# A delta-rule attention and a two-layer MoE in one kernel: the second layer with still tokens and moving weights, and a new order of norms, inversion and start

## The chip, the cores and the metric

The kernel runs on one core of one Trainium2 chip. The metric is the time of one execution on the device in microseconds (us). TensorE is called PE, VectorE DVE, ScalarE ACT, GpSimd POOL; SP is the engine that issues the DMAs here.

## The reference, cut to what matters

```python
# q, k, v: (4, 8, 768, 48); beta: (4, 8, 768); w_in: (384, 2048); w_out: (2048, 384)
k_n = k / (norm(k) + 1e-6)
for t in range(768):
    y[:, :, t] = q[:, :, t] @ state
    v_old = state.T @ k_n[t]
    state = state + beta[t] * outer(k_n[t], v[t] - v_old)
x = y.transpose(0, 2, 1, 3).reshape(3072, 384)
h = x @ w_in
g = maximum(h, 0) + log1p(exp(-abs(h)))
out = g @ w_out
```

## The kernel before, in words

**Attention.** The 768 tokens are cut into 12 chunks `s` of 64, two chunks make a pair `u`. All 32 heads of a chunk are worked on together, two heads side by side on the 128 partitions. For each pair the norms of k are taken (`norms`, L143: square on ACT, row sum on DVE L154, logarithm and exponential on ACT, then a chain of small DVE steps that ends with `cT`, `ncT`), the products k·k of each chunk (`gram`, L112), and the inverse of a unit lower triangular 32x32 matrix per head (`invert`, L180). The inversion is DVE work: one transposition (L193), two multiplications (L197, L199), then a step per column, each a multiplication into a scratch tile (L216) and an addition (L222). `finish` (L225) transposes the result twice (L228, L229). Pairs 0 and 1 invert 16x16 blocks and put them together on PE (`join`, L232). Then per chunk: `cross_a`, `cross_b`, `k_state`, `p_half` with `mask_p` (DVE L301), `u_all`, `y_all` (PE L333, then the split of y into two fp32r halves by ACT L337 and DVE L339, L341, then six small DMAs x<-x), and `state`.

**MoE.** Each chunk's 256 tokens go through both layers. The hidden 2048 features are 16 blocks `f`, taken two at a time, which is called a group here: eight groups per chunk. Numbers are kept as a sum of two fp32r parts, so each product is three matmuls. The first layer has w_in as the still operand and 256 token columns as the moving one, 18 matmuls per group (L428). ACT does three passes (L432 to L434), DVE three (L435, and the split into `gh` and `gl` by L438 and L439). The second layer (`outp`, L410) has 128 columns of w_out as the still operand and 256 token columns of `gh` or `gl` as the moving one, again 18 matmuls per group, into `po`, which holds the whole chunk in three banks. ACT copies `po` out and SP stores it. The first layer's PSUM tile `ph` has two buffers: a group's matmuls must wait until L435 of the group two before it is done.

**Weights.** They come as 64-bit floats. Each of the 16 blocks is converted by six DVE and ACT steps (`weights`, L354: ACT L366, DVE L372, L375, L378, L381, ACT L384, DVE L368, for the last block L386).

**Order.** Up to the end of the block at L508 the engines other than SP run in the order of the code. After it a planner writes the order: `attention` is a generator whose steps are let through by `attend` as the MoE goes on (`target`, with RATE, LEAD, FIRST), and a scheduler orders each engine's instructions from that. On each engine the instructions then run in that fixed order, SP's DMAs too. `prepare` (L464) did norms, gram and the whole inversion of the next pair in one go, after the even chunk. The tile `nv` (two buffers) holds v and, for the norms, k.

Of the kernel before, what the change touches and what calls it, by code (L numbers as in the profile page):

```python
# [34 lines left out]
def deltanet_moe(ctx, tc, kT, qT, kN, kI, vN, beta, wts, out):  # L35
# [7 lines left out]
    ps_a = E(tc.tile_pool(name="ps_a", bufs=3, space=PSUM))  # L43
# [68 lines left out]
    def gram(s):  # L112
        if s not in OFF:
            OFF[s] = two.tile([P, NP, HB], F32, name="off")
# [20 lines left out]
    def gram_below(s):  # L135
        OFF[s] = two.tile([P, NP, HB], F32, name="off")
# [6 lines left out]
    def norms(u, kas=None):  # L143

        ss = one.tile([P, 2 * NP], F32, name="ss")
        for j in range(2):
            if kas is None:
                ka = two.tile([P, NP, D], F32, name="nv")
                nc.sync.dma_start(ka, kN[2 * u + j])
            else:  # L150
                ka = kas[:, j]
            nc.scalar.activation(ka, ka, AF.Square)
            yield
            nc.vector.tensor_reduce(ss[:, j * NP:(j + 1) * NP], ka, op=ALU.add, axis=AX.X)  # L154
            yield
# [24 lines left out]
    def invert(u, cT, ncT):  # L180
# [22 lines left out]
        if u < N16:  # L203
# [5 lines left out]
            tmp = one.tile([P, HB, HB], F32, name="x0" if u == 0 else "x3")  # L209
        else:  # L210
            tmp = one.tile([P, HB, HB], F32, name="work")
# [113 lines left out]
    def y_all(s):  # L325
        x = X[s] = one.tile([P, 2, NK, B, C], F32R, name=f"x{s % 4}")
# [27 lines left out]
    def weights():  # L354
# [4 lines left out]
        ex = None  # L359
        for f in range(NF + 1):  # L360
            last, lastex = f - 1, ex
            if f < NF:
                w = ST[f].rearrange("p (n w) -> p n w", w=2)
                hw, lw = w[:, :, 1], w[:, :, 0]
                ex = two.tile([P, 2 * DM], I32, name="ex", bufs=3)
                nc.scalar.activation(ex.bitcast(F32), hw.bitcast(F32), AF.Abs)  # L366
                if f > 0:
                    nc.vector.tensor_tensor(W[last][:, 1], lastex.bitcast(F32), W[last][:, 0],  # L368
                                            op=ALU.subtract)
                    done[0] = f  # L370
                    yield
                nc.vector.tensor_scalar(ex.bitcast(F32), ex.bitcast(F32), 2.0 ** -15, 122880.0,  # L372
                                        op0=ALU.max, op1=ALU.min)
                yield
                nc.vector.tensor_scalar(ex, ex, 3, 0x3FFFFFF8, op0=ALU.logical_shift_left,  # L375
                                        op1=ALU.bitwise_and)
                yield
                nc.vector.scalar_tensor_tensor(ex, hw, -2 ** 30, ex, op0=ALU.bitwise_and,  # L378
                                               op1=ALU.bitwise_or)
                yield  # L380
                nc.vector.scalar_tensor_tensor(ex, lw, 29, ex, op0=ALU.logical_shift_right,  # L381
                                               op1=ALU.bitwise_or)
                W[f] = one.tile([P, 2, 2 * DM], F32R, name=f"w{f}")
                nc.scalar.copy(W[f][:, 0], ex.bitcast(F32))  # L384
            else:
                nc.vector.tensor_tensor(W[last][:, 1], lastex.bitcast(F32), W[last][:, 0],  # L386
                                        op=ALU.subtract)
                done[0] = f
            yield


    def moe():
# [115 lines left out]
    with tc.manual_schedule(engines={ET.PE, ET.DVE, ET.Activation, ET.Pool}):  # L508
# [6 lines left out]
        for f in range(2):  # L515
            load_weights(f)
# [174 lines left out]
```

## Time and profile before

| | us |
|---|---|
| median of 3 runs | 715.94 (714.91 to 717.95) |
| the profiled execution, its own time | 715.12 |
| its span in the profile | 713.4 |
| PE busy, matmuls | 621.8 |
| DVE busy | 452.6 |
| ACT busy | 351.7 |
| DVE busy, of the first 160 us | 120.0 |
| PE idle, of the first 80 us | 47.5 |

The span is what the profile covers of one execution; 1.7 us of the execution's own time lie outside it. Busy times of PE are modelled, since matmuls are pipelined, so its idle time is the better guide. A window row reads: from and to in us, its length, then for PE, PEld (the load of still operands), DVE, ACT and POOL the busy us and the number of instructions, the TensorE clock that was granted (1.00 is full), the DMA share and GB/s. A waits row reads: engine, line and tile that waited, on whom, us in total, how often, the longest.

### The profile page before, as it was taken

To read this page: it belongs to the slowest core of one execution; us is meant where nothing else is said; L and a number is where in the kernel's file an instruction comes from. 1 tells how busy PE (TensorE), PEld (TensorE's weight loads), DVE (VectorE), ACT (ScalarE), POOL (GpSimd) and SP (SyncE) were. 2 spreads that over 40 slices of the span, in tenths; PEclk is the share of its full clock that TensorE was granted. 3 is DMA by queue.
4 is the path that set the end of the run, shared out by engine and by line. 5 is a ranking of instruction groups with operands and counts; after the bars stand their busy time and mean duration, and the time that the engine had idled before them with its cause. 6 is when DMAs were issued, how large, how long until landed. Compare 5 with 4: busy or idle time off the path is not lost.

```text
span 713.4 us, 25301 instructions
## 1 busy us (share of the span) xinstructions
PE 621.8 (87%) x11392; PEld 594.9 (83%) x11392; DVE 452.6 (63%) x972; ACT 351.7 (49%) x651; POOL 28.5 (4%) x56
## 2 busy tenths in 40 slices
PE   3226879879998699999899999999798999999997
PEld 2226779778988698999799998899798989999996
DVE  1683799994454994465995449973679853534443
ACT  3304758634565246465346664463545555444443
POOL 4000000000000000000001000010000100000000
PEclk9999779899999899999999999999899999999999
DMA  9991212000042013041120312202302103000000
GB/s 245 374 374 35 58 45 59 1 1 27 3 112 59 1 46 79 2 119 53 46 57 26 106 44 69 57 2 91 79 3 48 55 3 80 2 12 23 2 23 22
DMA packets 36699, 45.36 MB, mean 64 GB/s; under 512 B 21648, under 2 KB 28688, under 8 KB 36592
## 3 DMA queue, kind: packets, MB, share of 16 engines
q1 hardware_dynamic: 36592, 43.76, 21.1%
q8 instruction: 89, 1.46, 0.9%
q14 instruction: 18, 0.15, 0.1%
HBM read 36.67 MB, written 4.72 MB: 58 GB/s over the span
## 4 chain that ended last, share of the span: by engine, by line
PE 57%; DVE 21%; ACT 9%; issue 7%; DMA 5%; SPq 1%; ACTq 0%; DVEq 0%
PE ph L428 21%; PE po L410 21%; PE pa L333 3%; DVE Z L222 3%; DVE work L216 2%; DMA nv<-kN 2%; PE pa L294 2%; DVE a L435 2%; PE pa L308 2%; ACT tt L265 1%; PE pa L320 1%; ACT a L432 1%; ACT a L433 1%; DVE gl L439 1%; PE pa L123 1%
## 5 line engine op out<-in xcount | busy, mean ns | idle before, releaser
L428 PE MATMUL ph<-x,w 128*128 128x256 f32 x1728 | 243.7, 293 | 20.1 <-DVE a L435 13.0
L428 PEld LDWEIGHTS ph<-x,w 128*128 128x128 f32 x1728 | 224.9, 197 | 24.3 <-DVE a L435 13.6
L410 PE MATMUL po<-gh,w 128*128 128x256 f32 x1152 | 179.1, 291 | 12.2 <-DVE gh L438 10.8
L410 PEld LDWEIGHTS po<-gh,w 128*128 128x128 f32 x1152 | 154.5, 193 | 16.0 <-DVE gh L438 9.6
L435 DVE SCALAR_TENSOR_TENSOR a<-ph,a 128x512 f32<-128x512 f32 x96 | 66.1, 689 | 158.0 <-ACT a L434 157.6
L432 ACT ACTIVATE a<-ph 128x512 f32<-128x512 f32 x96 | 57.2, 597 | 192.6 <-PE ph L428 185.9
L410 PE MATMUL po<-gl,w 128*128 128x256 f32 x576 | 103.1, 288 | 1.1 <-ACT ex L414 0.9
L410 PEld LDWEIGHTS po<-gl,w 128*128 128x128 f32 x576 | 84.0, 193 | 2.1 <-ACT ex L414 1.3
L439 DVE TENSOR_TENSOR gl<-a,gh 128x512 fp32r<-128x512 f32 x96 | 66.3, 690 | 4.2 <-PE po L410 1.8
L433 ACT ACTIVATE a<-a 128x512 f32<-128x512 f32 x96 | 60.5, 632 | 2.9
L434 ACT ACTIVATE a<-a 128x512 f32<-128x512 f32 x96 | 60.6, 632 | 2.7
L438 DVE CAST gh<-a 128x512 fp32r<-128x512 f32 x96 | 42.3, 441 | 7.4 <-PE po L410 4.0
L222 DVE TENSOR_TENSOR Z<-Z,work 128x30 f32<-128x30 f32 (+14 forms) x120 | 39.6, 330 | 2.9
L216 DVE TENSOR_TENSOR work<-Z,ltq 128x30 f32<-128x30 f32 (+14 forms) x120 | 39.5, 329 | 2.7
L333 PE MATMUL pa<-big 128*64 128x64 f32 x768 | 29.1, 235 | 4.3 <-DVE big L301 4.1
L333 PEld LDWEIGHTS pa<-big 128*64 128x64 f32 x768 | 26.5, 148 | 6.7 <-DVE big L301 4.6
L301 DVE TENSOR_TENSOR big<-pa,maskP 64x512 f32<-64x512 f32 x44 | 30.1, 685 | 0.8 <-PE pa L294 0.3
L323 ACT COPY big<-pa 48x384 f32<-48x384 f32 x44 | 20.8, 473 | 18.1 <-PE pa L320 17.4
L294 PE MATMUL pa<-big,kt 48*64 48x64 f32 x704 | 25.7, 224 | 3.1 <-ACT tt L277 2.3
L294 PEld LDWEIGHTS pa<-big,kt 48*64 48x64 f32 x704 | 23.2, 139 | 4.4 <-ACT tt L277 3.3
L267 POOL MEMSET tt<- 32x512 f32 x24 | 12.6, 524 | 311.2 <-ACT tt L265 201.3
L312 ACT COPY big<-pa 64x384 f32<-64x384 f32 x48 | 22.6, 470 | 3.2 <-PE pa L308 2.5
(96 smaller groups left out, 611.9 us busy)
## 6 DMA issues: line engine op xcount, KB each, us to landing
w<-wts SPq DMA_DIRECT2D x16, 768.0 KB, 13.2
kt<-kT SPq DMA_DIRECT2D x26, 192.0 KB, 4.4
big<-qT SPq DMA_DIRECT2D x24, 192.0 KB, 4.4
ki<-kI SPq DMA_DIRECT2D x24, 192.0 KB, 3.3
nv<-vN SPq DMA_DIRECT2D x12, 384.0 KB, 3.6
out<-ex SPq DMA_DIRECT2D x11, 384.0 KB, 2.6
nv<-kN SPq DMA_DIRECT2D x8, 384.0 KB, 3.5
x<-x SPq DMA_DIRECT2D x72, 32.0 KB, 2.0
```

The source lines that it names most:

```text
L216: nc.vector.tensor_tensor(tmp[:, a:a + r, 0:j], Z[:, a + j + 1:a + n, a + j:a + j + 1].to_broadcast([P, r, j]), lq[:, a + j:a + j + 1, a:a ...
L222: nc.vector.tensor_tensor(z, z, tmp[:, a:a + r, 0:j], op=ALU.add)
L294: nc.tensor.matmul(pt[tk[ab], i, :], kts[s % 3][dr[ab], 8 * g + i, :], bv[dr[ab], ab, 8 * g + i, 0:C], start=True, stop=True)
L333: nc.tensor.matmul(py[tk[ab], i, :], big[:, at + C:at + 2 * C], big[:, at:at + C], start=True, stop=True)
L410: nc.tensor.matmul(po[:, e, 0:n], W[f][:, a, DM + e * P:DM + (e + 1) * P], (gh, gl)[b][:, f - f0], start=(f == 0 and i == 0), stop=(f == N ...
L428: nc.tensor.matmul(ph[:, f - f0], W[f][:, a, k * P:(k + 1) * P], xr[b][k], start=(c == 0), stop=(c == 3 * NK - 1))
L432: nc.scalar.activation(a, ph, AF.Abs)
L433: nc.scalar.activation(a, a, AF.Exp, scale=-1.0)
L434: nc.scalar.activation(a, a, AF.Ln, bias=1.0)
L435: nc.vector.scalar_tensor_tensor(a, ph, 0.0, a, op0=ALU.max, op1=ALU.add)
L438: nc.vector.tensor_copy(gh, a)
L439: nc.vector.tensor_tensor(gl, a, gh, op=ALU.subtract)
```

## The change

Second layer: the still operand is now 128 of the chunk's tokens out of `gh` or `gl`, the moving one 384 columns of w_out. A block `f` takes 6 matmuls of 384 columns instead of 9 of 256. `po` needs two banks, the free one goes to the attention's pool `ps_a` (3 to 4 buffers). The last group of each chunk does one half of the tokens first, copies it out (128x384) and stores it, then the other.

Norms: the tile `nv` has three buffers. `chunk(s)` for even `s` from 2 on loads k and begins the norms of the next pair before its own work, ends them after the first `p_half`, and does the two grams of the next pair at its end. `load_v` is called a chunk earlier.

Inversion: it is handed to a list, `background`, from which the planner takes two pieces after each step of the MoE; what is left is taken when `finish` needs it. X has three buffers instead of four.

Start: the first inversion's norms, inversion and `finish` come without weight conversions between them; weight blocks 2 to 15 are loaded behind a small POOL memset of each (so after POOL's earlier work), pair 1's gram and norms are done in the start. The conversion steps are emitted in another order (the absolute value of the next block between two steps of this one, the subtraction of the last one after the second step).

```diff
-    ps_a = E(tc.tile_pool(name="ps_a", bufs=3, space=PSUM))
+    ps_a = E(tc.tile_pool(name="ps_a", bufs=4, space=PSUM))
...
-        NV[s] = two.tile([P, NP, D], F32, name="nv")
+        NV[s] = two.tile([P, NP, D], F32, name="nv", bufs=3)
...
+    def load_ka(s):
+        ka = two.tile([P, NP, D], F32, name="nv", bufs=3)
+        nc.sync.dma_start(ka, kN[s])
+        return ka
...
-        x = X[s] = one.tile([P, 2, NK, B, C], F32R, name=f"x{s % 4}")
+        x = X[s] = one.tile([P, 2, NK, B, C], F32R, name=f"x{s % 3}")
...
-            po = ps_o.tile([P, NK, 512], F32, name="po")
+            po = ps_o.tile([P, 2, 512], F32, name="po")
...
-                terms = [(f, i, e) for f in range(f0, f0 + 2) for i in range(3) for e in range(NK)]
-                last = f0 + 2 == NF and s == NS - 1
-                if last:
-                    terms.sort(key=lambda t: (t[1] == 2, t[2]))
+                terms = [(f, h, i) for f in range(f0, f0 + 2) for h in range(2) for i in range(3)]
                 if f0 + 2 == NF:
-                    ot = two.tile([P, NK, n], F32, name="ex", bufs=3)
+                    terms.sort(key=lambda t: t[1])
+                    ot = two.tile([P, 2, DM], F32, name="ex", bufs=3)
...
-                    nc.tensor.matmul(po[:, e, 0:n], W[f][:, a, DM + e * P:DM + (e + 1) * P],
-                                     (gh, gl)[b][:, f - f0], start=(f == 0 and i == 0),
+                    nc.tensor.matmul(po[:, h, 0:DM], (gh, gl)[b][:, f - f0, h * P:(h + 1) * P],
+                                     W[f][:, a, DM:], start=(f == 0 and i == 0),
...
+                    if f == NF - 1 and i == 2:
+                        nc.scalar.copy(ot[:, h], po[:, h, 0:DM])
+                        nc.sync.dma_start(out[s, h], ot[:, h])
...
     def chunk(s):
+        more = s % 2 == 0 and s + 2 < NS
         if s % 2 == 0:
             scale_v(s)
+            if more and s >= 2:
+                load_k(s + 2)
+                nm = norms(s // 2 + 1)
+                next(nm)
+            yield from begin(s)
         k_state(s)
         mask_p(0, p_half(s, 0))
         yield
+        if more and s >= 2:
+            cols[s // 2 + 1] = run(nm)
         u_all(s)
         mask_p(1, p_half(s, 1))
...
+        if more and s >= 2:
+            u = s // 2 + 1
+            systems(u)
+            load_k(s + 3)
+            gram(s + 2)
+            yield
+            gram(s + 3)
+            yield
+            background.append(invert(u, *cols[u]))
...
-        fill(2)
-        next(nm)
-        fill(2)
-        cols[0] = run(nm)
-        pts = [p_half(0, g, ps_h, "ph") for g in range(2)]
-        run(invert(0, *cols[0]))
+        pts = [p_half(0, g, ps_h, "ph") for g in range(2)]
         gram_below(1)
+        for f in range(2, NF):
+            ST[f] = one.tile([P, 4 * DM], I32, name=f"w{f}")
+            nc.gpsimd.memset(ST[f][:, 0:1], 0)
+            nc.sync.dma_start(ST[f], wts[f])
+            if f == 5:
+                load_k(3)
+        run(iv)
+        systems(1)
+        gram(2)
         finish(0)
...
+            if s % 2 == 0:
+                while background:
+                    yield "invert"
+                finish(s // 2)
+                yield
...
         while next(mg) != "chunk":
             groups += 1
+            invert_some(2)
             attend(0, target())
```

How the change moves DVE's instructions is shown at three places. In the rows a name is written ahead of `<-` and the names read behind it; numbers behind a name count tiles.

**DVE right after the first chunk's y.** Before, behind the last subtraction L341 of chunk 0 (`ex` and `w` are the conversion, `nv` is v, `a` the MoE):

```order
L91 TENSOR_TENSOR nv<-nv,nn 128x768
L378 SCALAR_TENSOR_TENSOR ex<-w_108,ex 128x768
L381 SCALAR_TENSOR_TENSOR ex<-w_108,ex 128x768
L368 TENSOR_TENSOR w_1047<-ex,w_1047 128x768
L372 TENSOR_SCALAR ex<-ex 128x768 x2
L375 TENSOR_SCALAR ex<-ex 128x768 x2
L372 TENSOR_SCALAR ex<-ex 128x768
L378 SCALAR_TENSOR_TENSOR ex<-w_110,ex 128x768
L378 SCALAR_TENSOR_TENSOR ex<-w_114,ex 128x768
L375 TENSOR_SCALAR ex<-ex 128x768
L381 SCALAR_TENSOR_TENSOR ex<-w_110,ex 128x768
L435 SCALAR_TENSOR_TENSOR a<-ph,a 128x512
```

In the change, six instructions behind the same subtraction (now L340), with the norms of pair 1 (`r_1125`) and, in L155, of pair 2:

```order
L383 SCALAR_TENSOR_TENSOR ex<-w_104,ex 128x768
L96 TENSOR_TENSOR nv<-nv,nn 128x768
L164 RECIPROCAL r_1125<-rt 128x32
L194 STREAM_TRANSPOSE ltq<-work 128x32x32
L165 TENSOR_TENSOR r_1125<-r_1125,ss 128x32
L166 TENSOR_TENSOR r_1125<-r_1125,rt 128x32
L155 TENSOR_REDUCE ss<-nv 128x16
L167 TENSOR_SCALAR nn<-r_1125 128x32
L171 TENSOR_TENSOR r_1125<-nn 128x32
L96 TENSOR_TENSOR nv<-nv,nn 128x768
L172 RECIPROCAL r_1125<-r_1125 128x32
L173 TENSOR_TENSOR r_1125<-r_1125,bet 128x32
```

The conversion of the third block stood here before; now the second block's stands among the norms of two pairs and the scaling of v, and the first L437 (L435 before) comes later in the list.

**DVE at the inversion of pair 2.** Before, from the L435 that precedes it:

```order
L435 SCALAR_TENSOR_TENSOR a<-ph,a 128x512
L193 STREAM_TRANSPOSE ltq<-work 128x32x32
L438 CAST gh<-a 128x512
L197 TENSOR_TENSOR ltq<-ltq,Z 128x1024
L439 TENSOR_TENSOR gl<-a,gh 128x512
L199 TENSOR_TENSOR Z<-ltq,cT 128x1024
L288 TENSOR_TENSOR nv<-nv,pa 128x8x48
L212 COPY Z<-cT 128x32
L216 TENSOR_TENSOR work<-Z,ltq 128x30
L288 TENSOR_TENSOR nv<-nv,pa 128x8x48
L222 TENSOR_TENSOR Z<-Z,work 128x30
```

In the change:

```order
L437 SCALAR_TENSOR_TENSOR a<-ph,a 128x512
L440 CAST gh<-a 128x512
L441 TENSOR_TENSOR gl<-a,gh 128x512
L194 STREAM_TRANSPOSE ltq<-work 128x32x32
L198 TENSOR_TENSOR ltq<-ltq,Z 128x1024
L200 TENSOR_TENSOR Z<-ltq,cT 128x1024
L211 COPY Z<-cT 128x32
L215 TENSOR_TENSOR work<-Z,ltq 128x30
L287 TENSOR_TENSOR nv<-nv,pa 128x8x48
L177 STREAM_TRANSPOSE cT<-r_4042 128x32
L221 TENSOR_TENSOR Z<-Z,work 128x30
```

The group's own casts moved ahead of the transposition; the inversion's first ten columns still follow in one stretch, with no MoE step among them.

**DVE at the norms of pair 3.** Before, from the second mask of the even chunk:

```order
L301 TENSOR_TENSOR big<-pa,maskP 64x8x64 x2
L154 TENSOR_REDUCE ss<-nv 128x16 x2
L159 TENSOR_SCALAR rt<-ss 128x32
L435 SCALAR_TENSOR_TENSOR a<-ph,a 128x512
L163 RECIPROCAL r_4569<-rt 128x32
L438 CAST gh<-a 128x512
L164 TENSOR_TENSOR r_4569<-r_4569,ss 128x32
L439 TENSOR_TENSOR gl<-a,gh 128x512
L165 TENSOR_TENSOR r_4569<-r_4569,rt 128x32
L339 TENSOR_TENSOR x_4373<-pa,x_4373 128x3x128
L341 TENSOR_TENSOR x_4374<-pa,x_4374 128x128
```

In the change, at the second mask of chunk 2:

```order
L300 TENSOR_TENSOR big<-pa,maskP 64x8x64 x2
L155 TENSOR_REDUCE ss<-nv 128x16 x2
L160 TENSOR_SCALAR rt<-ss 128x32
L164 RECIPROCAL r_4042<-rt 128x32
L165 TENSOR_TENSOR r_4042<-r_4042,ss 128x32
L338 TENSOR_TENSOR x_2769<-pa,x_2769 128x3x128
L340 TENSOR_TENSOR x_2770<-pa,x_2770 128x128
L166 TENSOR_TENSOR r_4042<-r_4042,rt 128x32
L96 TENSOR_TENSOR nv<-nv,nn 128x768
L437 SCALAR_TENSOR_TENSOR a<-ph,a 128x512
```

The same norms now stand one pair earlier, the two row sums still directly behind one another, and the next MoE step behind more of the chain than before.

More of the change, by code (lines that the diff above doesn't have):

```diff
@@ L135, in gram_below @@
     def gram_below(s):
-        OFF[s] = two.tile([P, NP, HB], F32, name="off")
+        OFF[s] = two.tile([P, NP, HB], F32, name="off", bufs=3)
         pas = [ps_a.tile([P, NP // 2, HB], F32, name="pa") for e in range(2)]
@@ L354, in weights @@
     def weights():
[L359 to L386, printed above, removed]
@@ new lines, in words, with magnitude @@
+        def words(f):
+            w = ST[f].rearrange("p (n w) -> p n w", w=2)
+            return w[:, :, 1], w[:, :, 0]
+        def magnitude(f):
+            ex = two.tile([P, 2 * DM], I32, name="ex", bufs=3)
+            nc.scalar.activation(ex.bitcast(F32), words(f)[0].bitcast(F32), AF.Abs)
+            return ex
+        ex, last = magnitude(0), None
+        yield
+        for f in range(NF):
+            hw, lw = words(f)
+            nc.vector.tensor_scalar(ex.bitcast(F32), ex.bitcast(F32), 2.0 ** -15, 122880.0,
+                                    op0=ALU.max, op1=ALU.min)
+            yield
+            nc.vector.tensor_scalar(ex, ex, 3, 0x3FFFFFF8, op0=ALU.logical_shift_left,
+                                    op1=ALU.bitwise_and)
+            yield
+            if f > 0:
+                nc.vector.tensor_tensor(W[f - 1][:, 1], last.bitcast(F32), W[f - 1][:, 0],
@@ L392, in moe @@
+            nc.scalar.copy(W[f][:, 0], ex.bitcast(F32))
+            last, ex = ex, after
+            yield
+        nc.vector.tensor_tensor(W[NF - 1][:, 1], last.bitcast(F32), W[NF - 1][:, 0],
+                                op=ALU.subtract)
+        done[0] = NF
+        yield
     def moe():
@@ L533, in deltanet_moe @@
                                     base=-QB, pattern=[[0, 1]], channel_multiplier=1)
-        nc.gpsimd.memset(Z, 0.0)
-        nc.gpsimd.memset(big[:, 2 * NP * QW:], 0.0)
+        systems(0)
+        nm = norms(0, kas[0])
+        for _ in range(5):
+            next(nm)
+        gram_diagonal(0, ps_a, "pa")
+        gram_diagonal(1, ps_a, "pa")
+        cols[0] = run(nm)
+        iv = invert(0, *cols[0])
+        next(iv)
         nc.gpsimd.memset(maskP, 1.0)
@@ L571, in deltanet_moe @@
         cross_b(0)
-        fill(2)
+        nm = norms(1, kas[1])
+        next(nm)
+        next(nm)
         u_all(0)
@@ L575, in deltanet_moe @@
         next(jn)
-        fill(3)
+        next(nm)
+        next(nm)
         run(jn)
@@ L583, in deltanet_moe @@
         load_v(1)
+        next(nm)
+        fill(5)
         scale_v(1)
+        gram(3)
+        cols[1] = run(nm)
+        cross_b(1)
         fill(5)
@@ L623, in attend @@
                 return
-            units += 1
+            if r == "invert":
+                if steps_done >= steps:
+                    return
+                invert_some(1)
+            else:
+                units += 1
     def target():
@@ L688 @@
     r = _run(nc, [data], core_ids=[0])
[L689 removed]
+    o = r.results[0]["out"].reshape(NS, B, C, DM).transpose(1, 0, 2, 3)
     return np.ascontiguousarray(o).reshape(NT, DM)
```

109 lines of the change are left out of this document (45 added, 64 removed).

## The prediction

> **What bounds the kernel now.** I read the page first, then busy time by stage (windows), then the waits, then the timeline of the start.
>
> ```profile
> span 713.4 us, 25301 instructions
> PE 621.8 (87%) x11392; PEld 594.9 (83%) x11392; DVE 452.6 (63%) x972; ACT 351.7 (49%) x651; POOL 28.5 (4%) x56
> PE 57%; DVE 21%; ACT 9%; issue 7%; DMA 5%; SPq 1%; ACTq 0%; DVEq 0%
> ```
>
> PE carries over half of the chain that ended last, DVE a fifth. Where each of them does so is seen by stage:
>
> ```profile
> 0.00:80.00 80.00, 32.47 (x1349) 29.71 (x1350) 41.91 (x120) 27.54 (x54) 12.26 (x30) 1.00 0.73 237
> 80.00:160.00 80.00, 69.11 (x958) 63.87 (x957) 78.11 (x164) 47.75 (x81) 0.63 (x2) 0.81 0.11 29
> ...
> 220.00:250.00 30.00, 23.36 (x313) 22.48 (x313) 23.89 (x55) 9.02 (x16) 0.00 (x0) 0.84 0.06 21
> ...
> 495.00:512.00 17.00, 12.90 (x144) 12.30 (x139) 8.94 (x22) 7.44 (x17) 1.27 (x1) 0.80 0.39 104
> ...
> 630.00:713.40 83.40, 78.35 (x652) 77.52 (x651) 32.49 (x55) 35.82 (x59) 0.00 (x0) 1.00 0.05 15
> ```
>
> In the first 80 us nothing is full: chunk 0's attention is one chain over DMA, DVE, ACT and PE. From 80 to 160 DVE is busy 78.1 of 80 us: it converts the weights, and PE, which depends on it, runs at a granted clock of 0.81. After 160 PE is the bound, but for a few holes: 6.6 us idle at 220 to 250, 4.1 us at 495 to 512 (each with a low clock behind it, 0.84 and 0.80). What opens them, the waits say:
>
> ```profile
> PE ph L428 <- DVE a L435: 13.0, 4, 5.9
> ...
> PE po L410 <- DVE gh L438: 10.8, 8, 4.1
> ...
> DVE ss L154 <- ACT nv L152: 21.7, 8, 6.6
> ...
> PE ph L428 <- DMA x<-x: 4.8, 5, 2.6
> ```
>
> The longest of the first row (5.9) is the inversion of pair 2, which keeps DVE from L435. The longest of the second (4.1) is at 504 us, where DVE stood 6.6 us before a row sum of the norms, whose k had not landed, with the casts queued behind it.
>
> So a change gains where it takes PE work away, closes such a hole, or lets DVE end the conversions sooner.
>
> **The second layer.** Three steps of the chain at full clock give the pace:
>
> ```profile
> 402.55 2.13 PE po L410 x18
> 404.68 2.02 PE pa L333 x64
> ...
> 411.22 1.57 PE pa L320 x64
> ```
>
> A matmul of 256 columns takes 2.13/18 = 118.3 ns. One of 64 columns takes 31.6 ns, one of 48 takes 24.5 ns: 0.44 ns per column. By that slope 384 columns take 118.3 + 128 x 0.44 = 174.6 ns (an estimate; no row has 384). 12 x 16 x 9 = 1728 matmuls become 1152: 204.4 us become 201.1, a gain of 3.3 us of PE time, all of it on PE's path. From both sides: by columns alone (177.5 ns) nothing; with a whole short matmul of 24.5 ns as the fixed part saved 576 times, 14.1 us. I take 3.3, since the two short rows give the slope directly.
>
> The Trainium skill (TensorE: Matmul & The Clock Gate, Back-to-back issue gap) puts an isolated gap at columns/2.4 + 2.5 ns, so 162.5 ns for 384 columns and 109.2 for 256; by its 162.5 against the measured 118.3 the gain would be 17.2 us and the sum 693. The trace speaks against taking it as it stands: 256 columns cost 118.3 ns here, not 109.2.
>
> **The start.** Its rows, from the chain and the timeline:
>
> ```profile
> 15.69 5.39 issue
> ...
> 47.25 3.62 issue
> ```
>
> ```profile
> 11.35 0.18 DVE L159 TENSOR_SCALAR rt<-ss 128x32 f32<-128x32 f32 x1
> ...
> 29.23 2.09 DVE L193 STREAM_TRANSPOSE ltq<-work 128x1024 f32<-128x1024 f32 x1
> ...
> 43.97 1.87 DVE L229 STREAM_TRANSPOSE tt<-Z 128x1024 f32<-128x1024 f32 x1
> ```
>
> ```profile
> 74.25 0.28 DVE L341 TENSOR_TENSOR x<-pa,x 128x128 fp32r<-128x128 f32 x1
> ...
> 158.25 1.98 DVE L229 STREAM_TRANSPOSE tt<-Z 128x1024 f32<-128x1024 f32 x1
> ```
>
> The norms' row sums are there at 11.35, but the inversion starts at 29.23, since DVE's list has conversion steps in between that wait for a weight block. Without them the norms' short steps end about 3 us after 11.35. The inversion took 29.23 to 45.84 with pair 1's row sums in it, 14.6 us without the two, so it now ends at 29. From its end to the last subtraction of chunk 0's y lie 28.7 us, of them 3.6 in which PE stood for nothing that the profile names ("issue"); the other such stall, 5.4 us, falls into the time when the weights landed. The chain now runs while 14 weight blocks land, so I count the larger stall's 5.4 us on top of the 25.1 us of work, though others may be hidden: y's last subtraction comes at 59.5, 15 us earlier.
>
> From there to the end of pair 1's inversion (160.2, L229) DVE is full: 85.7 us before. What its list holds there in the change differs by these prices:
>
> ```profile
> L381 DVE SCALAR_TENSOR_TENSOR ex<-w,ex 128x768 int32<-128x768 int32 x16 | 15.3, 954 | 0.1
> L368 DVE TENSOR_TENSOR w<-ex,w 128x768 fp32r<-128x768 f32 x15 | 14.3, 958 | 8.9 <-ACT w L384 8.9
> ...
> L91 DVE TENSOR_TENSOR nv<-nv,nn 128x768 f32<-128x768 f32 x12 | 11.4, 951 | 3.3 <-DMA nv<-vN 3.3
> ...
> L372 DVE TENSOR_SCALAR ex<-ex 128x768 f32<-128x768 f32 x16 | 8.9, 556 | 12.9 <-ACT ex L366 12.9
> ...
> L375 DVE TENSOR_SCALAR ex<-ex 128x768 int32<-128x768 int32 x16 | 8.7, 552 | 0.1
> L154 DVE TENSOR_REDUCE ss<-nv 128x16 f32<-128x768 f32 x8 | 7.6, 952 | 21.7 <-ACT nv L152 21.7
> ...
> L163 DVE RECIPROCAL r<-rt 128x32 f32<-128x32 f32 x6 | 2.1, 343 | 0.0
> ```
>
> ```profile
> L439 DVE TENSOR_TENSOR gl<-a,gh 128x512 fp32r<-128x512 f32 x96 | 66.3, 690 | 4.2 <-PE po L410 1.8
> L435 DVE SCALAR_TENSOR_TENSOR a<-ph,a 128x512 f32<-128x512 f32 x96 | 66.1, 689 | 158.0 <-ACT a L434 157.6
> ...
> L438 DVE CAST gh<-a 128x512 fp32r<-128x512 f32 x96 | 42.3, 441 | 7.4 <-PE po L410 4.0 <-PE pa L239 1.2
> ```
>
> ```profile
> 120.53 0.95 DVE L378 SCALAR_TENSOR_TENSOR ex<-w,ex 128x768 int32<-128x768 int32 x1
> 121.39 0.95 DVE L368 TENSOR_TENSOR w<-ex,w 128x768 fp32r<-128x768 f32 x1
> ```
>
> More conversion, since less was done before the inversion: one L372, two L375, one each of L378 and L381 (0.95 each), two L368: 5.5 us. Two scalings of v more: 1.9 us. The norms of pair 2 and the rest of pair 1's: two row sums (1.9 us) and 17 short steps (4.2 us, an estimate at 0.25 each, between L159's 0.18 and L163's 0.34). Fewer: two groups of the MoE, 2 x 1.82 = 3.6 us. Together 9.9 us, and as steps that follow at once overlap a little (0.95 us long, 0.86 from start to start at 120.53), 8.9 us of time. So the inversion of pair 1 ends at 160.2 - 15 + 8.9 = 154.1, 6.1 us sooner, with two MoE groups fewer done, which PE must still do: 2 x 36 x 118.3 ns = 8.5 us. The start thus costs 2.4 us on balance, though the first MoE matmul comes some 15 us sooner. Bounds: -6.1, if PE has idle time later for those groups, and +17, if chunk 0's chain gains nothing. I take +2.4, as PE is full after 160.
>
> **The norms.** They are begun a pair earlier, but their two row sums still stand behind one another on DVE, and the second k load waits for DVE again (the two loads go through one buffer, as the other two hold v). Before, at pair 3:
>
> ```profile
> 306.99 0.95 DVE L154 TENSOR_REDUCE ss<-nv 128x16 f32<-128x768 f32 x1 [0.75 <-ACT nv L152]
> 311.81 0.95 DVE L154 TENSOR_REDUCE ss<-nv 128x16 f32<-128x768 f32 x1 [3.87 <-ACT nv L152]
> ```
>
> So the wait of some 4 us stays, with the L437 of the next group and ACT's passes queued behind it. It opened a hole on PE only where PE had no other work: at 495 to 512 (4.1 us idle and 0.2 x 12.9 = 2.6 us of clock) and about 1 us for pair 2. Now pair 2's falls into the start, and behind the others stand two more groups of MoE work. I count 1.2 us each for the three left: 7.7 - 3.6 = 4.1 us gained. Bounds: 7.7 gained, or 12 lost if each of the three costs the worst one's 6.7.
>
> **The inversion.** The pieces are handed out two at a time, yet DVE's list shows the first ten columns in one stretch. Before, two L435 around pair 2's stood here:
>
> ```profile
> 225.03 0.69 DVE L435 SCALAR_TENSOR_TENSOR a<-ph,a 128x512 f32<-128x512 f32 x1 [9.83 <-ACT a L434]
> ...
> 239.16 0.69 DVE L435 SCALAR_TENSOR_TENSOR a<-ph,a 128x512 f32<-128x512 f32 x1
> ```
>
> 14.1 us lie between them. In the new list the stretch between the two holds about as much DVE work, and its transposition still waits for the gram. Only the casts go ahead, which gives PE one group of the second layer to do. I take 1.5 us off the hole of 5.9 and nothing off the later ones; bounds 9 (all such holes after 160 closed) and -6 (each as deep as this one).
>
> **Small ones.** The waits of L428 for x after 160 are 4.8 less the two of the start:
>
> ```profile
> 78.34 0.59 PE L428 MATMUL ph<-x,w 128*128 128x256 f32 x3 [2.62 <-DMA x<-x]
> 79.53 0.98 PE L428 MATMUL ph<-x,w 128*128 128x256 f32 x3 [0.60 <-DMA x<-x]
> ```
>
> 1.6 us, gained, since two groups of the MoE now stand on PE between y of chunk 2 and its first use. The last group needs `gl` at its third matmul instead of its thirteenth: L439's 0.69 us less 2 x 0.17, 0.3 us lost at the end. The output copies grow from 11 large and 3 small to 24 of middle size, off the path, as ACT is half idle. X's third buffer and the one for `ps_a` I cost at nothing: y is written after the MoE is through with the chunk three before.
>
> **The sum.** 713.4 - 3.3 + 2.4 - 4.1 - 1.5 - 1.6 + 0.3 = 705.6 of span, and with the 1.7 us outside it 707.3, say 707. That stands to the profiled execution's 715.1; the median shown is 715.9, 0.8 above it.
>
> **Rivals.**
> - *The earlier start counts in full* (-6.1 instead of +2.4): 699. For it: DVE has under half its time busy in 0 to 80. Against it: PE has no idle time after 160 in which to do two groups.
> - *The fixed part of a matmul goes* at 384 columns, where a load hides wholly behind the stream: 384 x 0.44 = 169 ns, 194.7 us, 9.7 gained instead of 3.3: 701. Against it: a 64-column matmul with its load takes only 31.6 ns.
> - *The holes stay*: norms, inversion and x each open as much as before, a wait in the place of each: 707 + 7.2 = 714; with nothing from the second layer 718. For it: the lists still hold the same stretches.
> - *Slower: the first chain is caught in the weights.* I count six stretches of 128 small matmuls between the inversion and y, and suppose that each begins with a stall like the two quoted. If each adds 3.6 us to the 25.1 of work while the 14 blocks land, y comes at 29 + 25.1 + 21.6 = 75.7, 16 us later than I say: 723. For it: the two rows of issue. Against it: such a stall is hidden where PE waits for DVE or ACT anyway. It decides from a y at 72 us on.
>
> **How the numbers follow.** Forecast (700 to 713) 0.48, early start 0.12, fixed part 0.07, holes stay 0.20, slower start 0.13. Under half a per cent (3.6 us about 715.9) a measurement of this kernel can't tell from no change, so faster means below 712.3. Faster: 0.45 of the forecast, 0.12 and 0.07, 0.64. Same: the rest of the forecast and the holes, 0.23. Slower: 0.13. The range from 692 (the two gains together) to 719 leaves out the slow start and a little of the rest.
>
> **What would show it.** Right: 18-odd microseconds between the first row sum and `finish`, y of chunk 0 near 59, the end of pair 1's inversion near 154; groups of 12 second-layer matmuls in 2.1 us; L155 with a wait of some 4 us before its second; a hole of 4 to 5 us at pair 2's inversion. Wrong: second layer groups well under 2.0 us, PE full from 60 us on, or y of chunk 0 after 65.

## The result: slower by 2.35%

| | before | after |
|---|---|---|
| median, us | 715.95 (714.91 to 717.95, 4 runs) | 733.01 (731.89 to 734.08, 4 runs) |
| ratio | | 1.0235, 95% interval 1.0207 to 1.0262 |
| span of the profiled execution | 713.4 | 730.2 |

The forecast was 707 in a range of 692 to 719. From the page of the changed kernel:

```profile
span 730.2 us, 24225 instructions
PE 634.9 (87%) x10816; PEld 596.5 (82%) x10816; DVE 459.2 (63%) x972; ACT 354.1 (48%) x661; POOL 31.3 (4%) x70
PE 52%; DVE 29%; issue 7%; DMA 6%; ACT 5%; POOL 1%; SPq 0%; DVEq 0%; ACTq 0%; POOLq 0%
```

PE carries less of the chain than before, DVE 8 points more. By stage:

```profile
0.00:80.00 80.00, 42.84 (x1731) 39.06 (x1731) 41.34 (x112) 31.49 (x66) 12.27 (x42) 0.95 0.78 243
80.00:160.00 80.00, 56.23 (x475) 49.72 (x475) 79.23 (x178) 42.95 (x66) 3.23 (x4) 0.75 0.13 32
...
200.00:250.00 50.00, 42.84 (x764) 39.88 (x761) 32.78 (x74) 23.70 (x50) 0.00 (x0) 0.87 0.22 61
...
400.00:450.00 50.00, 45.49 (x938) 42.47 (x932) 23.06 (x42) 25.09 (x52) 0.00 (x0) 0.93 0.22 58
450.00:500.00 50.00, 47.51 (x544) 44.60 (x537) 45.28 (x104) 22.91 (x42) 1.27 (x1) 0.93 0.17 45
```

In the first 80 us PE is busy 10 us more than before. From 80 to 160 DVE is as full as before, and PE is busy 13 us less at a clock of 0.75 instead of 0.81. After 200 us PE stands over 2 us at a time at six places, before at four. Two sums over such rows show how: PE's idle time, and the clock lost while it is busy (busy time by one less the granted clock, summed over 0 to 160, 160 to 200 and then every 50 us; good to some 2 us, as the clock has two digits).

| us | idle to 200 | clock lost to 200 | idle after 200 | clock lost after 200 |
|---|---|---|---|---|
| before | 60.3 | 11.7 | 31.3 | 8.6 |
| after | 64.5 | 18.1 | 30.8 | 15.6 |
| after, three PSUM buffers (below) | 63.2 | 18.3 | 21.6 | 5.2 |
| all mends (below) | 55.6 | 19.0 | 16.6 | 0.0 |

After 200 us the change has as much idle time as before, but in pieces that cost more clock; up to 200 both are worse.

**The start.** DVE in chunk 0 and at the end of pair 1's inversion (L160 follows the row sums, L194 opens the inversion, L228 ends it, L340 is y's subtraction):

```profile
11.20 0.18 DVE L160 TENSOR_SCALAR rt<-ss 128x32 f32<-128x32 f32 x1
...
14.60 2.07 DVE L194 STREAM_TRANSPOSE ltq<-work 128x1024 f32<-128x1024 f32 x1 [0.33 <-ACT work L110]
...
28.31 1.88 DVE L228 STREAM_TRANSPOSE tt<-Z 128x1024 f32<-128x1024 f32 x1
...
66.70 0.28 DVE L340 TENSOR_TENSOR x<-pa,x 128x128 fp32r<-128x128 f32 x1
...
160.90 1.86 DVE L228 STREAM_TRANSPOSE tt<-Z 128x1024 f32<-128x1024 f32 x1
```

The inversion ends at 30.2 (I said 29), but y at 67.0 instead of 59.5, and pair 1's inversion at 162.8 instead of 154.1. The chain of waits says where y's 7.5 us went. These are all its steps over 1 us between 30 and 67 that are called "issue", that is, in which PE waited for nothing that the profile names:

```profile
30.21 3.16 issue
...
36.02 5.35 issue
...
44.41 3.15 issue
...
60.05 1.08 issue
```

12.7 us, where I had counted 5.4. What they are, the DMA rows of three of these windows show (30.2 to 33.4, 36 to 41.4, 44.4 to 47.6):

```profile
q8 instruction: 1, 0.02, 2.1%
...
q8 instruction: 1, 0.02, 1.3%
...
q8 instruction: 1, 0.02, 2.2%
```

In each stall one packet of 16 KB, marked as instructions, moves on queue 8; the fourth stall stands right behind one. PE goes on 1.3 to 1.6 us after that packet has ended. So in these places PE waits for its own instructions.

Further on PE waits for converted weights (L389 and L378 write the two parts of a block), 21.4 us in all against 2.4 before:

```profile
PE ph L430 <- ACT w L389: 13.9, 8, 4.4
...
PE ph L430 <- DVE w L378: 7.5, 7, 2.0
```

**The second layer** runs at the pace that I gave it, 12 matmuls of 384 columns in 2.09 us, 174.2 ns each:

```profile
519.95 2.09 PE po L415 x12
```

By the formula of the Trainium skill (TensorE: Matmul & The Clock Gate, Back-to-back issue gap) an isolated one would take 162.5 ns, an estimate; here the measurement differs and decides.

**The norms.** DVE and SP at the norms of pair 5 (L155 row sum, L96 scaling of v, L437 and L440 the MoE):

```profile
412.87 0.95 DVE L155 TENSOR_REDUCE ss<-nv 128x16 f32<-128x768 f32 x1 [0.27 <-ACT nv L153]
418.11 0.95 DVE L155 TENSOR_REDUCE ss<-nv 128x16 f32<-128x768 f32 x1 [4.29 <-ACT nv L153]
...
423.18 0.96 DVE L96 TENSOR_TENSOR nv<-nv,nn 128x768 f32<-128x768 f32 x1 [2.10 <-DMA nv<-vN]
...
424.66 0.69 DVE L437 SCALAR_TENSOR_TENSOR a<-ph,a 128x512 f32<-128x512 f32 x1
425.39 0.43 DVE L440 CAST gh<-a 128x512 fp32r<-128x512 f32 x1
```

```profile
408.57 0.34 SPq L92 DMA_DIRECT2D nv<-kN  x1
...
413.85 0.35 SPq L92 DMA_DIRECT2D nv<-kN  x1
...
419.09 0.35 SPq L88 DMA_DIRECT2D nv<-vN  x1
```

```profile
425.87 1.01 PE L415 MATMUL po<-w,gh 128*128 128x384 f32 x2 [4.45 <-DVE gh L440]
```

Three loads go one after the other through one buffer. The third, v's, is new in this place: it can start only when the second row sum is done (419.06), and L96, which needs it, stands ahead of the MoE's L437 in DVE's list. PE waits 4.45 us for the cast behind it, and its clock is 0.66 from 422 to 432. The same place costs PE 3.54 us at pair 4 and 2.11 at pair 3.

**The inversion** of pair 2 in DVE's list, from the casts of one group to the L437 of the next, and PE behind it:

```profile
223.25 0.69 DVE L437 SCALAR_TENSOR_TENSOR a<-ph,a 128x512 f32<-128x512 f32 x1 [3.94 <-ACT a L436]
...
230.26 2.05 DVE L194 STREAM_TRANSPOSE ltq<-work 128x1024 f32<-128x1024 f32 x1 [5.13 <-ACT work L110]
...
243.80 0.69 DVE L437 SCALAR_TENSOR_TENSOR a<-ph,a 128x512 f32<-128x512 f32 x1
```

```profile
244.55 4.21 PE L430 MATMUL ph<-x,w 128*128 128x256 f32 x18 [2.98 <-DVE a L437]
```

20.6 us between two L437, where 14.1 lay between the two L435 before: DVE first waits for the gram with nothing else in hand, then does ten columns in one stretch. PE stands 2.98 us instead of 5.91, but from 230 to 250 its clock is 0.67. Half of that low clock is not the hole's doing: the clock is 0.50 from 230 to 236.5 already, behind an "issue" stall of 1.74 us that ends at 228.7, and again from 243.5 to 250. Pairs 3, 4 and 5 cost 2.89, 2.28 and 0.93 us; before, 3.13, 1.14 and 2.47.

### The profile page after: what moved, and what is told of

Same layout as the page of the kernel before. It is cut to its first block, busy times and chain, and to the rows that moved or that the text cites. A ratio compares the mean times of both kernels' runs of the same rounds, so it can differ in the third digit from the quotient of the medians.

```text
span 730.2 us, 24225 instructions
## 1 busy us (share of the span) xinstructions
PE 634.9 (87%) x10816; PEld 596.5 (82%) x10816; DVE 459.2 (63%) x972; ACT 354.1 (48%) x661; POOL 31.3 (4%) x70
## 3 DMA queue, kind: packets, MB, share of 16 engines
q8 instruction: 85, 1.39, 0.8%
## 4 chain that ended last, share of the span: by engine, by line
PE 52%; DVE 29%; issue 7%; DMA 6%; ACT 5%; POOL 1%; SPq 0%; DVEq 0%; ACTq 0%; POOLq 0%
PE po L415 20%; PE ph L430 18%; DVE work L215 4%; DVE Z L221 3%; DMA nv<-kN 3%; DVE a L437 3%; DMA big<-qT 2%; PE pa L255 2%; PE pa L332 2%; DVE gh L440 2%; DVE gl L441 2%; DMA nv<-vN 2%; DVE w L378 1%; PE pa L307 1%; DVE ex L383 1%
## 5 line engine op out<-in xcount | busy, mean ns | idle before, releaser
L430 PE MATMUL ph<-x,w 128*128 128x256 f32 x1728 | 249.2, 296 | 29.2 <-ACT w L389 13.9
L430 PEld LDWEIGHTS ph<-x,w 128*128 128x128 f32 x1728 | 234.5, 201 | 35.7 <-ACT w L389 15.9
L415 PE MATMUL po<-w,gh 128*128 128x384 f32 x768 | 209.1, 354 | 16.2 <-DVE gh L440 15.2
L437 DVE SCALAR_TENSOR_TENSOR a<-ph,a 128x512 f32<-128x512 f32 x96 | 66.1, 690 | 166.2 <-ACT a L436 158.8
L415 PEld LDWEIGHTS po<-w,gh 128*128 128x128 f32 x768 | 138.9, 196 | 21.4 <-DVE gh L440 15.2
L415 PE MATMUL po<-w,gl 128*128 128x384 f32 x384 | 134.6, 350 | 0.2
L415 PEld LDWEIGHTS po<-w,gl 128*128 128x128 f32 x384 | 75.1, 195 | 2.2 <-DVE gl L441 1.6
L435 ACT ACTIVATE a<-a 128x512 f32<-128x512 f32 x96 | 60.8, 633 | 2.9
L440 DVE CAST gh<-a 128x512 fp32r<-128x512 f32 x96 | 44.2, 461 | 12.4 <-PE po L415 5.0
L215 DVE TENSOR_TENSOR work<-Z,ltq 128x84 f32<-128x84 f32 (+14 forms) x148 | 44.2, 306 | 2.8
L221 DVE TENSOR_TENSOR Z<-Z,work 128x84 f32<-128x84 f32 (+14 forms) x148 | 44.1, 306 | 2.9
L300 DVE TENSOR_TENSOR big<-pa,maskP 64x512 f32<-64x512 f32 x44 | 30.2, 686 | 2.0 <-PE pa L293 1.5
L322 ACT COPY big<-pa 48x384 f32<-48x384 f32 x44 | 20.9, 475 | 20.6 <-PE pa L319 20.0
L293 PE MATMUL pa<-big,kt 48*64 48x64 f32 x704 | 28.2, 232 | 1.5 <-issue 0.9
L258 ACT ACTIVATE off<-pa 32x512 f32<-32x512 f32 x24 | 14.1, 586 | 18.9 <-PE pa L255 18.6
## 6 DMA issues: line engine op xcount, KB each, us to landing
w<-wts SPq DMA_DIRECT2D x16, 768.0 KB, 14.1
```

Source lines behind the costliest of these rows:

```text
L215: nc.vector.tensor_tensor(tmp[:, a:a + r, 0:j], Z[:, a + j + 1:a + n, a + j:a + j + 1].to_broadcast([P, r, j]), lq[:, a + j:a + j + 1, a:a ...
L221: nc.vector.tensor_tensor(z, z, tmp[:, a:a + r, 0:j], op=ALU.add)
L293: nc.tensor.matmul(pt[tk[ab], i, :], kts[s % 3][dr[ab], 8 * g + i, :], bv[dr[ab], ab, 8 * g + i, 0:C], start=True, stop=True)
L415: nc.tensor.matmul(po[:, h, 0:DM], (gh, gl)[b][:, f - f0, h * P:(h + 1) * P], W[f][:, a, DM:], start=(f == 0 and i == 0), stop=(f == NF - ...
L430: nc.tensor.matmul(ph[:, f - f0], W[f][:, a, k * P:(k + 1) * P], xr[b][k], start=(c == 0), stop=(c == 3 * NK - 1))
L435: nc.scalar.activation(a, a, AF.Exp, scale=-1.0)
```

## The experiments

Ratios are to runs of the kernel before on the same chip, with 95% intervals. Beside the experiments the kernel before ran at medians of 717.3 to 718.9, one to three us above the first runs, so times of different experiments are compared by their ratios.

**The second layer alone**, in the kernel before (the `outp` of the change, `po` with two banks, `ps_a` still with three buffers).

> The kernel before with nothing changed but the second layer: 384 moving columns, po in two banks, the last group of a chunk in two halves (ps_a stays at 3 buffers). Theory A (the second layer gives what its pace gives): the changed kernel shows 2.08 to 2.11 us for 12 matmuls, 174.5 ns each, so 204.4 us become 201.0, and the time is 716.0 - 3.4 + 0.3 = about 713. Rival B (the second layer is what made the change slow, by its order of matmuls or its waits for gl): above 720.

719.05, ratio 1.0023 (0.9989 to 1.0057): neither; theory A's 713 would be 0.996. The groups show the pace (12 matmuls in 2.11 us), but there is no gain, and not even PE's busy time shows the 3.3 us:

```profile
PE 621.0 (87%) x10816; PEld 580.3 (81%) x10816; DVE 452.5 (63%) x972; ACT 352.0 (49%) x661; POOL 28.5 (4%) x56
```

It is 621.0 us against 621.8, at a higher mean clock (0.977 against 0.962), and PE is idle 1.2 us longer. Its waits for `gl` grow from 0.2 to 2.6 us and those for ACT's copies of `po` from 0.9 to 3.2, while those for L435 (L431 there) shrink from 13.0 to 9.0. Where the rest of the pace goes is not shown.

**The norms' k in tiles of its own.**

```diff
     def load_ka(s):
-        ka = two.tile([P, NP, D], F32, name="nv", bufs=3)
+        if s < 6:
+            ka = two.tile([P, NP, D], F32, name="nv", bufs=3)
+        else:
+            ka = one.tile([P, HB, HB], F32, name=("ltq", "work")[s % 2])
+            ka = ka.rearrange("p a b -> p (a b)")[:, 0:NP * D].rearrange("p (q d) -> p q d", d=D)
         nc.sync.dma_start(ka, kN[s])
...
+        if u > 2:
+            kas = [load_ka(2 * u), load_ka(2 * u + 1)]
```

> The changed kernel, but the k of the norms of pairs 3 to 5 is loaded into the inversion's two scratch tiles (idle between two inversions), both loads at once, and no longer through the buffer that v needs as well. Theory A (three loads one after the other through one buffer, each waited for by DVE with the casts of the MoE behind it, are what made the norms costly): the PE waits for L440 of 2.1, 3.5 and 4.5 us go, with the low clock behind them; PE lost about 2.8, 4.9 and 7.2 us there, so 733 becomes 720 to 724. Rival B (PE has too little queued there in any case and the hole only moves, to the inversion or to y): 730 to 733.

717.77, ratio 1.0022 (0.9996 to 1.0049): 2.1% below the change, some 15 us; theory A, and by more than its sum, with a list that is written anew here as well. The norms of pairs 4 and 5 open no hole on PE any more, those of pair 3 one of 2.54 us. The inversions still do (2.56 us at 242, 2.85 at 346, 2.28 at 449).

**v apart from k**, with as much memory as the change.

```diff
-        NV[s] = two.tile([P, NP, D], F32, name="nv", bufs=3)
+        NV[s] = two.tile([P, NP, D], F32, name="nv")
...
-        ka = two.tile([P, NP, D], F32, name="nv", bufs=3)
+        ka = one.tile([P, NP, D], F32, name="ka")
```

> The changed kernel with the three buffers of nv split by use: two for v, one for the norms' k; as much memory. Theory A (v's load waits for a buffer that k holds until the second row sum, and DVE's v scaling, with the MoE's casts behind it, waits for that load): the waits of L96 go and the time is 717 to 724. Rival B (the wait before the second row sum, for the second k through the one buffer, is what costs, as it does in the kernel before): it stays, and the time is 730 to 733.

719.47, ratio 1.0061 (1.0025 to 1.0096): theory A by its time, and DVE's waits of L96 for v fall from 5.2 to 1.1 us. Only the sharing was undone; the two k loads still follow one another through one buffer. But the order changed too: with a buffer that v does not hold, the row sums moved far ahead to where DVE has other work (pair 5's between the inversion steps of pair 2 at 239 and 244, with waits of 0 and 0.77 us). So rival B's wait went as well, and this run doesn't tell the two waits apart.

**Weight blocks 4 to 15 later.** Their loop of memset and load stands behind `arrange(1)`:

```diff
-        for f in range(2, NF):
+        def load_behind(f):
...
-            if f == 5:
-                load_k(3)
+
+        for f in range(2, 4):
+            load_behind(f)
+        load_k(3)
...
         arrange(1)
+        for f in range(4, NF):
+            load_behind(f)
         state(0)
```

> The changed kernel, but weight blocks 4 to 15 are loaded only behind POOL's memset of the second chunk's arrange, that is when chunk 0's y is nearly through; blocks 2 and 3 stay. Theory A (the nameless stalls of PE in chunk 0's chain, 13.3 us between the end of the inversion and y, come from the weights that land at the same time): stalls fall to 1 to 2 us each, the last subtraction of y comes at 58 to 60 instead of 67, the end of pair 1's inversion 6 to 8 us sooner, and the time is 725 to 728. Rival B (the stalls are there without the weights too): y stays at 66 to 67 and the time at 733, or above if DVE now waits for weights.

721.31, ratio 1.0078 (1.0046 to 1.0111): theory A, and by more. All "issue" of 0.4 us or more in the chain from 28 to 60, and the two marks on DVE:

```profile
29.73 3.44 issue
...
35.81 1.24 issue
...
40.09 0.40 issue
```

```profile
59.64 0.28 DVE L340 TENSOR_TENSOR x<-pa,x 128x128 fp32r<-128x128 f32 x1
...
154.72 1.87 DVE L228 STREAM_TRANSPOSE tt<-Z 128x1024 f32<-128x1024 f32 x1
```

The stalls fall to 5.1 us, y comes 7.1 us earlier, pair 1's inversion ends 6.2 us earlier. The first stall stays (3.44 us); the second falls from 5.35 to 1.24. In the change the 16 KB packet of the second started 2.8 us into the stall, while the DMA moved 353 GB/s (36 to 41.4 us); here it starts 1.5 us ahead of the stall, at 22 GB/s (29.7 to 37.1). This fits bulk loads that hold up the packet; the first stall isn't theirs. The gain of 11 us is more than that; the rest lies in later holes, in a list that the scheduler wrote anew, and is not explained by the stalls.

**The old start**, first with its three more steps that the planner counts, then with the same number as the change (the lines that bear on the steps, without the first block and the conversion's order, which are those of the kernel before; the first version has a `yield` behind `cross_b(1)`, `gram(2)` and `gram(3)` besides).

```diff
+        cross_b(1)
         k_state(1)
...
+        cols[1] = run(norms(1, kas[1]))
+        systems(1)
+        gram(2)
+        load_k(3)
+        gram(3)
         background.append(invert(1, *cols[1]))
```

> The changed kernel with the start of the kernel before: its first block, its order of the conversion steps, cross_b, norms and grams of pair 1 back in the attention; second layer, norms, inversion in pieces as in the change. Theory A (the start costs the change 9.3 us: the inversion of pair 1 ends 0.8 us later than before, with two groups or 8.5 us of MoE work fewer done by then): 724. Rival B (the start costs the 2.4 us of the prediction, and the loss is all in the norms and inversions): 730 to 731.

765.64, ratio 1.0668 (1.0627 to 1.0709): neither theory. Three steps more put the attention later against the MoE through the whole kernel, as the next run shows by leaving them out. This one says nothing of the start.

> The last experiment's old start again, but with cross_b and the two grams of pair 1 as part of a neighbouring step, so that the planner, which counts the attention's steps against the MoE's groups, counts as many of them as in the change (the run before had three more, each of which put the attention later). Theory A (the start costs the change 9 us and the 765 came from the three steps): 722 to 726. Rival B (the start costs 2 to 3 us): 730 to 731. Rival C (the rest of the change is built on the new start, and with the old one the attention is late however its steps are counted): above 740.

734.17, ratio 1.0215 (1.0183 to 1.0246): as slow as the change. By its time it is none of the three, by the ratio 731 at the level of the first runs (729 to 734), where rival B lies. Here y comes at 79.8 and pair 1's inversion ends at 160.1, but as few MoE groups are done by then as in the change (9 of the first layer, 5 of the second), since the norms of pair 2 and the scalings of v stand in DVE's list ahead of it with this start as well. y comes 12.8 us later than in the change, and still the inversion ends 2.7 us earlier, as DVE converts weights during the chain. I read this as DVE's work up to there being what counts, and y's time only as far as DVE idles for it.

**Both mends** together (k in the scratch tiles, weights late).

> The changed kernel with both mends: k of pairs 3 to 5 in the inversion's scratch tiles, weight blocks 4 to 15 behind the second chunk's arrange. Theory A (two causes in different stretches, so their gains of 15 and 12 us add): 705 to 708, faster than both kernels. Rival B (both give back the same holes, PE having as much MoE work left to do in either): 712 to 717.

710.48, ratio 0.9885 (0.9857 to 0.9913): faster than both kernels, 1.2% faster than the one before. By ratios the gains of 2.1% and 1.6% add to 3.5 of 3.7, and the time is 708 at the first runs' level: theory A.

**Both mends, and pair 2's norms behind pair 1's inversion** (`s < 4`, `u > 1` in the first diff).

> The kernel with both mends (710.5 measured), with pair 2's norms too through the inversion's scratch tiles, so that they can run only behind pair 1's inversion: 2 row sums and some 8 short DVE steps, 3 to 4 us, leave the stage in which DVE is the bound. Theory A (what the start costs is DVE work ahead of the end of pair 1's inversion): 706 to 708. Rival B (then pair 2's inversion comes later, and PE waits for it instead): 711 to 716.

702.88, ratio 0.9837 (0.9788 to 0.9885), which is 707 if 0.9885 stands for 710.5: theory A. Pair 1's inversion ends 4.3 us earlier than with both mends alone (at 152.0, not 156.3), as much as the steps taken out of the stage.

```profile
150.15 1.87 DVE L234 STREAM_TRANSPOSE tt<-Z 128x1024 f32<-128x1024 f32 x1
```

**The inversion in one go**, in the change (pair 1's in the same way).

```diff
-            background.append(invert(u, *cols[u]))
+            run(invert(u, *cols[u]))
```

> The changed kernel with each inversion emitted in one go where the change puts it on its list. Theory A (pieces change little, since DVE's list has the first ten columns in one stretch either way): 731 to 735. Rival B (pieces do close the holes of PE at the inversion): 738 or more. Rival C (pieces cost time, since the inversion ends later and the next pair's chain with it): below 729.

734.43, ratio 1.0230 (1.0202 to 1.0258): theory A, the pieces are worth nothing in the change.

**The old second layer** in the change, which brings `ps_a` back to three buffers, as `po` takes three banks.

> The changed kernel with the second layer of the kernel before (256 moving columns, po in three banks, ps_a with three buffers). Theory A (the second layer is worth its pace wherever PE is full): 733 + 3 to 5 = 736 to 738. Rival B (as in the kernel before with the new second layer alone: what PE gains in its groups it waits for in the next hole, so nothing): 732 to 734. Rival C (the new second layer or the fourth buffer costs time): below 731.

724.02, ratio 1.0078 (1.0053 to 1.0103): rival C. So either the matmuls or the buffers cost time, which the next run tells apart.

**Three buffers in `ps_a`**, all else as in the change.

```diff
-    ps_a = E(tc.tile_pool(name="ps_a", bufs=4, space=PSUM))
+    ps_a = E(tc.tile_pool(name="ps_a", bufs=3, space=PSUM))
```

> The changed kernel with three buffers in the attention's PSUM pool as before (the second layer stays new; one bank unused). In DVE's list of it the L437 of the next group stands ahead of v's scaling L96 at the norms of pairs 4 and 5, in the change behind it. Theory A (the 9 us that the old second layer gave back came from DVE's order at the norms, which the fourth buffer had turned, not from the matmuls): 722 to 727. Rival B (they came from the new second layer's own matmuls): 731 to 735.

716.12, ratio 1.0014 (0.9976 to 1.0052): more than theory A asked for. The one number takes back all that the change lost. With it the scheduler writes another list; that the list makes the difference, and not the buffer in itself, is argued from the rows below, as no run keeps one list with both counts. DVE with three, at pair 5's norms:

```profile
407.47 0.95 DVE L155 TENSOR_REDUCE ss<-nv 128x16 f32<-128x768 f32 x1 [4.33 <-ACT nv L153]
...
409.42 0.69 DVE L437 SCALAR_TENSOR_TENSOR a<-ph,a 128x512 f32<-128x512 f32 x1 [0.78 <-ACT a L436]
...
410.28 0.36 DVE L440 CAST gh<-a 128x512 fp32r<-128x512 f32 x1
...
412.05 0.96 DVE L96 TENSOR_TENSOR nv<-nv,nn 128x768 f32<-128x768 f32 x1 [0.68 <-DMA nv<-vN]
```

The waits of DVE are the same (4.33 us for the second k, 0.68 for v), but L437 and the cast stand ahead of L96, and PE waits 1.41 us, not 4.45. At pair 2's inversion:

```profile
233.50 0.69 DVE L437 SCALAR_TENSOR_TENSOR a<-ph,a 128x512 f32<-128x512 f32 x1 [6.02 <-ACT a L436]
234.10 2.04 DVE L194 STREAM_TRANSPOSE ltq<-work 128x1024 f32<-128x1024 f32 x1
236.04 0.39 DVE L440 CAST gh<-a 128x512 fp32r<-128x512 f32 x1
...
242.52 0.69 DVE L437 SCALAR_TENSOR_TENSOR a<-ph,a 128x512 f32<-128x512 f32 x1
```

9.0 us between two L437 instead of 20.6, the casts between them, and no hole of over 0.8 us on PE there. By the table above most of the gain is behind 200 us: 9.2 us less idle time and 10.4 us less lost to the clock. Why the scheduler writes this list with three buffers and the other with four stays open.

**Three buffers, the inversion in one go.**

> The changed kernel with three buffers in ps_a (716.1 measured) and each inversion emitted in one go. Theory A (the pieces do close holes, but only with three buffers, where DVE's list has MoE steps among them; with four, taking the pieces away changed 733.0 to 734.4): 721 to 728. Rival B (pieces are worth nothing with three buffers either): 714 to 718.

725.25, ratio 1.0102 (1.0057 to 1.0147): theory A, 0.9% or 6 us against the run before. So the pieces gain something here, where the list puts MoE steps among them, and nothing in the change, where it doesn't.

**All mends**: the kernel of 702.88 with three buffers.

> The kernel with all mends so far (k of pairs 2 to 5 in the scratch tiles, weights late; 702.9 measured) with three buffers in ps_a instead of four. Theory A (the fourth buffer costs at the inversions too, whose first ten columns DVE's list then holds in one stretch, with no MoE step among them, as in the change; with three it has them among the MoE's steps): 694 to 699. Rival B (its cost was all at the norms, which are mended here): 701 to 705.

700.48, ratio 0.9752 (0.9716 to 0.9787), the fastest kernel here, 2.5% below before and 4.7% below the change. By the ratio that is 698 at the first runs' level: theory A, the fourth buffer costs at the inversions too. At pair 2's inversion 12.0 us lie between two L443 (L437 in the change) instead of 19.0 with four buffers, and PE stands 1.57 us instead of 4.25. Its clock, in 40 slices of 17.4 us, stays full from the eleventh on:

```profile
PEclk9998578868999999999999999999999999999999
```

**All mends with the old second layer.**

> The same as the first of this call (all mends, three buffers), with the second layer of the kernel before. Theory A (where the holes are small, the new second layer is worth its pace: 1152 matmuls of 174 ns against 1728 of 118.3, some 4 us): 3 to 6 us above the first run of this call. Rival B (worth nothing, as in the kernel before alone): within 2 us of it. Rival C (costs time): below it.

717.22, ratio 0.9987 (0.9957 to 1.0017): 2.3% or some 17 us above, four times the pace and more than theory A or either rival has. Both mends with the old layer and three buffers had shown the same sign:

> The kernel with both mends (710.5 measured), with the second layer of the kernel before and three buffers in ps_a. Theory A (with the holes small, PE is the bound and the new second layer is worth its pace, 3 to 5 us): 713 to 716. Rival B (the new second layer costs time in any surroundings, as the 9 us gained without it might say): 706 or less. Rival C (worth nothing, as in the kernel before): 709 to 712.

714.18, ratio 0.9984 (0.9949 to 1.0018), against 0.9885 with the new one and four buffers: in theory A's range by its time, by the ratios rather more, 7 us. So the new second layer was worth nothing in the kernel before, 0.6% in the change with three buffers (1.0014 against 1.0078), and 2.3% here. Its own part by the pace is about 3.3 us. In the last pair the traces put nearly all of their 20 us into holes and clock: with the old layer PE is idle 9.7 us longer and loses 11 us more to its clock, summed as in the table. The list is written anew for each (with the old layer DVE stands 9.0 us ahead of pair 2's inversion for the gram, and PE 3.07 us at 239 and 4.48 at 273). That the list makes all of this difference is argued, not shown.

## Why the prediction was wrong

- **The buffer costed at nothing** is the step that failed most. "X's third buffer and the one for `ps_a` I cost at nothing": the reason given there holds for X alone, and taking the fourth buffer away gives back 2.2%, the whole loss. X's third buffer was not tried alone. With three buffers the kernel stands at 717 by the ratio, still 10 us above the forecast; that is left to the steps below. I asked what a free buffer does for the instruction that waits for it, not what it does to the written order of all others.
- **Norms**: "I count 1.2 us each for the three left", a gain of 4.1. I had v's scaling ahead of the MoE step in the rows of the order, and did not ask when its load can start. PE stands 2.11, 3.54 and 4.45 us there, at clocks down to 0.66 behind. Undoing the sharing gives 12 to 15 us, part of which is other order.
- **Inversion**: a gain of 1.5 was forecast with "bounds 9 and -6". The four holes are 9.1 us in sum against 12.7 before, 3.6 less, but the clock around them is lower (0.67 against 0.83 from 230 to 250, and 0.66 from 460 to 470), which takes it back. That the list held the first ten columns in one stretch was read rightly.
- **Start**: forecast as a cost of 2.4, it comes to about 11 by the same count: pair 1's inversion ends 2.6 us later than before, not 6.1 sooner, and 8.4 us of MoE work fewer are done by then (162 matmuls of the first layer instead of 195, 3.9 us; in the second 60 x 174.2 ns instead of 126 x 118.3, 4.5 us), which is the two groups of my text. The interval from y to that end, 95.8 us, was right (94.6); y was 7.5 us late: the inversion took 15.6 us where I had 14.6 (14.7 by the rows), and I counted one stall at the larger size, 5.4 us, and found four, 12.7; the work of the chain was 1 us shorter. This was the mechanism of my slower rival at about half its size: it had y at 75.7, measured 67.0, while I had set 72 as the point from which it decides. It cost time with less already, and others came on top. Later weights give back 11 us, but the old start gives back nothing in the change (1.0215), since in the new order it reaches no more groups; so the 11 us are not the start's alone.
- **Second layer**: the pace of 174.6 ns was right (174.2). The step "all of it on PE's path" failed: alone in the kernel before it gained nothing, in time or in PE's busy time.
- **x and the end**: the waits of L430 for x are gone, as said (1.6). The wait of PE at the last group is 1.12 us against 1.07; the 0.3 lost there can't be told from nothing.
- **The sum** added terms of a kernel whose order I held fixed. Each edit here rewrites the lists: a buffer count alone moved the time by 16 us, three counted steps alone by 32 (1.0668 against 1.0215), without any change of work. So the shares above overlap: 16, 12 to 15 and 11 us are more than the 17 that the change lost and the 26 that the forecast missed, and they can't be added up to a cause of each us.

The packets of the instruction stalls have a row on the page as well:

```profile
q8 instruction: 85, 1.39, 0.8%
```

1.39 MB in 85 packets is 16.4 KB each; the Trainium skill (Runtime: NRT & Kernel Launch, Terms) says that an engine's instructions are refilled in blocks of 16 KiB, with which the row agrees.

## What to carry to other kernels

Where a scheduler writes the order, a pool's buffer count is an edit of the whole program: compare the written lists at the places where the bound engine waits, and try the count by itself before crediting or blaming the change beside it. A load through a shared buffer inherits the waits of all who hold it, and the engine that waits for it makes everybody queued behind it wait too. Here an early start would have gained only without a bulk load beside its instructions that could come later, and without more work in the stage that bounds.

## What the runs showed of the hardware

**Instructions.** In the traces before and after, PE has 16 stalls of over 0.9 us that the profile calls "issue". Every one of them ends 1.2 to 1.7 us behind the end of a 16 KB packet of the instruction queue, which itself takes some 1.1 us. The longest (5.39 us before, 5.35 after) stand where that packet started 2.8 us into the stall, while other loads moved.

**The clock.** After 200 us the granted clock fell behind each hole of 2.28 us or more on PE but one, in the kernels before and after (0.66 from 460 to 470 behind 2.28 us; one of 2.47 before showed none), and with all mends, whose longest hole there was 1.72 us, it stayed at 1.00 in all rows of 50 us. This is no threshold: in other runs it stayed up behind 3.04 us (the old start with the steps counted, at 424), and it fell behind 1.74 us (the change, at 229) and 1.96 us (three buffers, at 313). By the table the change lost 7 us more than before to its clock after 200 us, at equal idle time.
